# Softmax of a fused sparse-attention and cosine-FFN kernel: lasting exponential tiles with a column of 1e-9, and exponentials of the first local units straight from PSUM

## The chip, the core and the metric

The kernel runs on one core of one Trainium2 chip. The core has five engines that work side by side, each issuing its own instructions in order: PE (TensorE, matrix products), DVE (VectorE), ACT (ScalarE), POOL (GpSimd) and SP (SyncE, which here only issues transfers). Transfers (DMA) run beside them, issued by SP and by ACT. SBUF is the on-chip memory of 128 partitions; PSUM holds the results of PE, in eight banks of 512 fp32 columns.

The metric is the device time of one launch in microseconds. The kernel before has a median of 1000.85 us over three runs (1000.22 to 1001.1).

## The reference

Eight batches, eight heads, 576 positions, head size 64. Heads 0 to 3 attend to the last 32 positions, heads 4 to 7 to every 32nd position behind. The output becomes `x` with 4608 tokens of 512 features, and goes through a feed-forward layer with `h * cos(h)`.

```python
def _attn_ref(q, k, v):
    B, H, S, D = q.shape                                  # 8, 8, 576, 64
    stride = 32
    scores = (1.0 / np.sqrt(D)) * np.matmul(q, k.transpose(0, 1, 3, 2))
    pos = np.arange(S)
    rel = pos[:, None] - pos[None, :]
    mask_local = (rel >= 0) & (rel < stride)
    mask_strided = (rel >= 0) & (pos[None, :] % stride == pos[:, None] % stride)
    masks = np.stack([mask_local if h < H // 2 else mask_strided for h in range(H)], axis=0)
    scores = np.where(masks[None, :, :, :], scores, -1000000000.0)
    scores = scores - np.max(scores, axis=-1, keepdims=True)
    attn = np.exp(scores)
    attn = attn / (np.sum(attn, axis=-1, keepdims=True) + 1e-09)
    return np.matmul(attn, v).astype(np.float32)

def _moe_ref(x, w_in, w_out):                             # 4608x512, 512x2048, 2048x512
    h = x @ w_in
    g = h * np.cos(h)
    return (g @ w_out).astype(np.float32)

x = attn_out.transpose(0, 2, 1, 3).reshape(B * S, H * D)
return _moe_ref(x=x, **moe_kwargs)
```

## The kernel before

**Attention units.** A batch is ten units. Four are *strided* (head pairs p = 0, 1; halves u = 0, 1): six groups of 54 queries by 54 keys for each of two heads or half groups, a score tile of 128 x 324. Six are *local* (u = 0 to 2, p = 0, 1): three blocks of 64 queries by 96 keys for two heads, a score tile of 128 x 288. The zeros and minus infinities of the masks come as constants. A unit is a Python generator with three stages, which `step` calls one at a time:

1. loads of queries, keys and values (SP: L238, L240 local; L276, L278 strided), the mask and the scores on PE (L184; L249 local, L290 strided), and the softmax (L195 to L228) on DVE, ACT and POOL;
2. transposes on PE (L257 local, L302 strided) and a copy to `pt` on ACT (L259, L306);
3. products with the values on PE (L265, L316), copies to `x_l` or `x_t` on ACT (L269; L322, L328), and a transfer to `xT` in DRAM, issued by ACT (L271, L333).

**The softmax** has two forms. In the *plain* one, for batches 0 and 1 (20 units), the mask is added by a matmul into PSUM; DVE takes the maximum of each row and block and subtracts it (L199, L200), ACT takes the exponential into `e_sb` (L212, Exp). In the *later* one, for batches 2 to 7 (60 units), which runs beside the feed-forward layer whose ACT function is Sin, the exponential is made of two Silu, one DVE combination and a Square (L204 to L219), and POOL does the subtraction (L206). In both, DVE sums each block (L221, to `z`), adds 1e-9 (L222) and takes the reciprocal (L223); POOL multiplies by it (L225). Local units multiply in place in `e_sb`. Strided ones write to one of two lasting tiles `pn_s`, 128 x 6 x 64, whose columns 54 to 63 stay zero, since their transposes take 64 columns of each group.

**Feed-forward.** The 4608 tokens are 12 blocks of 384, the 2048 hidden features 16 chunks of 128. `load_x` brings a block of `xT` back in four pieces (SP L347 to `x_raw`) and splits each in a high and a low part (DVE L348, POOL L349). A chunk is `hidden`: twelve matmuls (L358), then ACT L364 (h / 2 pi, rounded), DVE L365 (the reduced argument), ACT L368 (Sin), DVE L371 (times h), ACT L374 and POOL L375 (the split `g_hi`, `g_lo`); and `outer`, three chunks later (`LAG`): nine matmuls (L382) into three accumulators of 128 x 512. After the last chunk of a block these go to `o` tiles (ACT, DVE, ACT: L390, L392) and to DRAM (SP L393).

**Order of the program.**

- First the 20 plain units, with warm-up matmuls between them (`keep_busy`, L442). `load_x(0)` and `load_x(1)` are written at steps 12 and 20.
- Then the weights, 32 tiles of 512 KB in two buffers `raw`: transfer (SP L114), DVE L116 and L119, ACT L124, DVE L125, ACT L129, and POOL L130, which frees the buffer. L116 of chunk f may not come ahead of L365 of chunk f - 2 of block 0 (`order` with `reduced`). Blocks 0 and 1 are computed as the weights come, and the first three chunks of block 2.
- Then blocks 2 to 11, with the 60 later units between the chunks, at places that a table (`KNOTS`) gives.

Up to block 2 a scheduler with a model of the time sets the order of each engine's instructions, within the dependences; a change of the code there also moves others. From block 2 on, PE's matmuls keep the order in which they are written (`in_turn`). `tile_pool` gives buffers in rotation: an instruction that writes a buffer waits for the last reader of what was in it. Plain units have three banks for scores (two of pool `ps_h`, one of `ps`), four `e_sb`, two `t_sb` and three `qk` buffers. `o` has two buffers up to the third chunk of block 2, so for the copies of blocks 0 and 1, and three behind it (pools `op`, L462 and L480).

Of the kernel before, what the change touches and what calls it, by code (L numbers as in the profile page):

```python
# [24 lines left out]
P = 128  # L25
# [4 lines left out]
LU = 3  # L30
# [38 lines left out]
def attention_cos_ffn(ctx, tc, qkl, vl, qkvs, w_in, w_out, eye, eye16, mask_l0, mask_l, mask_s, out):  # L69
# [85 lines left out]
    class Attention:  # L155
# [3 lines left out]
        def __init__(self, stack, plain, scores, transposed, products, ld_bufs):  # L159
# [11 lines left out]
            self.pn_s = itertools.cycle(pn_s)  # L171
# [23 lines left out]
        def softmax(self, s, mask, n, w, pn=None):  # L195
            t = self.wk.tile([P, SU * GB], F32, name="t_sb")[:, :n * w].rearrange("p (t w) -> p t w", w=w)
            mx = sm.tile([P, SU], F32, name="mx")
            if self.plain:
                nc.vector.tensor_reduce(out=mx[:, :n], in_=s, op=ALU.max, axis=AX.X)  # L199
                nc.vector.tensor_tensor(  # L200
                    out=t, in0=s, in1=mx[:, :n].unsqueeze(2).broadcast_to([P, n, w]), op=ALU.subtract
                )
            else:
                nc.vector.tensor_tensor(out=t, in0=s, in1=mask, op=ALU.add)  # L204
                nc.vector.tensor_reduce(out=mx[:, :n], in_=t, op=ALU.max, axis=AX.X)  # L205
                nc.gpsimd.tensor_tensor(  # L206
                    out=t, in0=t, in1=mx[:, :n].unsqueeze(2).broadcast_to([P, n, w]), op=ALU.subtract
                )
            e = self.wk.tile([P, SU * GB], F32, name="e_sb", bufs=4 if self.plain else 3)
            e = e[:, :n * w].rearrange("p (t w) -> p t w", w=w)  # L210
            if self.plain:
                exps.append(nc.scalar.activation(out=e, in_=t, func=AF.Exp, scale=0.125))  # L212
            else:
                nc.scalar.activation(out=e, in_=t, func=AF.Silu, bias=shift1, scale=0.0625)  # L214
# [378 lines left out]
```

## Time and profile before

| | us |
|---|---|
| median of three runs | 1000.85 (1000.22 to 1001.1) |
| profiled execution | 999.46 |
| its span, first to last instruction | 997.7 |
| PE busy | 968.3 (97%) |
| PE weight loads, beside PE | 847.5 (85%) |
| DVE busy | 466.5 (47%) |
| ACT busy | 499.2 (50%) |
| POOL busy | 385.2 (39%) |

The mean granted clock of TensorE was 0.995. Shares over the whole span average stages with different limits; here follows how the span divides. Plain attention fills the time to about 54 us, when the twelfth matmul of the first hidden chunk ends; until 205 us the weights stream in; at about 223 us the softmax of the first later unit is at its sums; from 256 us on blocks and later units alternate; and the last block's `o` goes out at the end. Rows of the timeline give the start in microseconds from the start of the span, the duration, the engine and line, the operation, output and inputs, and in brackets for how long the engine had waited and for what. A `q` behind an engine's name is its queue of transfers. In a row of waits stand the waiting instruction, the releaser, and then the total in us, the number of waits and the longest. In a row of groups stand the count, the busy time in us, the mean in ns of one, and the idle time ahead of them. In a row of a stretch stand its length, then for each engine its busy time and instructions.

### The profile page before, as it was taken

To read this page: it belongs to the slowest core of one execution; us is meant where nothing else is said; L and a number is where in the kernel's file an instruction comes from. 1 tells how busy PE (TensorE), PEld (TensorE's weight loads), DVE (VectorE), ACT (ScalarE), POOL (GpSimd) and SP (SyncE) were. 2 spreads that over 40 slices of the span, in tenths; PEclk is the share of its full clock that TensorE was granted. 3 is DMA by queue.
4 is the path that set the end of the run, shared out by engine and by line. 5 is a ranking of instruction groups with operands and counts; after the bars stand their busy time and mean duration, and the time that the engine had idled before them with its cause. 6 is when DMAs were issued, how large, how long until landed. Compare 5 with 4: busy or idle time off the path is not lost.

```text
span 997.7 us, 17749 instructions
## 1 busy us (share of the span) xinstructions
PE 968.3 (97%) x6890; PEld 847.5 (85%) x6890; DVE 466.5 (47%) x1005; ACT 499.2 (50%) x1043; POOL 385.2 (39%) x418
## 2 busy tenths in 40 slices
PE   8988988998999999999999999999999999999998
PEld 5777877877888888888888888888888888889997
DVE  6866677655454444434344444444344444322222
ACT  3655555565555555455445545554454544433433
POOL 2555554544344344333333344434243333332221
PEclk9999999999899999999999999999999999999999
DMA  8963333232322222111211322211221310100000
GB/s 247 300 199 103 111 108 112 80 105 73 102 85 88 70 79 84 42 50 59 83 58 35 110 79 76 82 50 53 88 59 34 98 55 29 41 20 1 33 1 32
DMA packets 48228, 80.14 MB, mean 80 GB/s; under 512 B 5904, under 2 KB 33296, under 8 KB 48144
## 3 DMA queue, kind: packets, MB, share of 16 engines
q1 hardware_dynamic: 38208, 69.35, 23.1%
q10 hardware_dynamic: 9936, 9.65, 2.8%
q8 instruction: 54, 0.88, 0.4%
q14 instruction: 30, 0.25, 0.1%
HBM read 60.11 MB, written 18.87 MB: 79 GB/s over the span
## 4 chain that ended last, share of the span: by engine, by line
PE 78%; DMA 4%; DVE 2%; ACT 1%; issue 1%; POOL 0%; DVEq 0%; POOLq 0%; ACTq 0%; SPq 0%
PE h L358 35%; PE acc L382 34%; DMA raw<-in_w_out 2%; PE acc L249 2%; PE acc L265 2%; PE acc L316 2%; PE acc L290 2%; PE acc L257 1%; PE acc L302 1%; DVE raw L116 1%; DMA raw<-in_w_in 1%; DMA xT<-x_t 0%; ACT r L368 0%; DVE r L371 0%; DVE raw L119 0%
## 5 line engine op out<-in xcount | busy, mean ns | idle before, releaser
L375 POOL TENSOR_TENSOR g_lo<-r,g_hi 128x384 fp32r<-128x384 f32 x192 | 198.3, 1033 | 396.6 <-issue 249.2
L358 PE MATMUL h<-x_hi,wi_h 128*128 128x384 f32 x768 | 267.9, 349 | 13.7 <-DVE r L371 13.7
L358 PE MATMUL h<-x_hi,wi_l 128*128 128x384 f32 x768 | 259.7, 338 | 0.0
L358 PE MATMUL h<-x_lo,wi_h 128*128 128x384 f32 x768 | 259.4, 338 | 0.0
L365 DVE SCALAR_TENSOR_TENSOR r<-r,h 128x384 f32<-128x384 int32 x192 | 106.1, 552 | 270.8 <-ACT r L364 247.7
L382 PE MATMUL acc<-wo_l,g_hi 128*128 128x512 f32 x576 | 227.4, 395 | 0.0
L382 PE MATMUL acc<-wo_h,g_hi 128*128 128x512 f32 x576 | 224.2, 389 | 1.4 <-ACT g_hi L374 1.4
L382 PE MATMUL acc<-wo_h,g_lo 128*128 128x512 f32 x576 | 224.6, 396 | 0.0
L358 PEld LDWEIGHTS h<-x_hi,wi_h 128*128 128x128 f32 x768 | 145.2, 189 | 31.0 <-DVE r L371 19.8
L368 ACT ACTIVATE r<-r,quarter 128x384 f32<-128x384 f32 x192 | 118.5, 617 | 96.5 <-DVE r L365 96.2
L358 PEld LDWEIGHTS h<-x_lo,wi_h 128*128 128x128 f32 x768 | 145.3, 189 | 5.0
L371 DVE TENSOR_TENSOR r<-r,h 128x384 f32<-128x384 f32 x192 | 106.0, 552 | 84.0 <-ACT r L368 83.4
L358 PEld LDWEIGHTS h<-x_hi,wi_l 128*128 128x128 f32 x768 | 145.1, 189 | 0.1
L364 ACT ACTIVATE r<-h 128x384 int32<-128x384 f32 x192 | 93.4, 487 | 102.0 <-PE h L358 95.5
L374 ACT CAST g_hi<-r 128x384 fp32r<-128x384 f32 x192 | 98.3, 512 | 87.5 <-DVE r L371 87.2
L382 PEld LDWEIGHTS acc<-wo_h,g_lo 128*128 128x128 f32 x576 | 108.0, 188 | 22.8
L382 PEld LDWEIGHTS acc<-wo_h,g_hi 128*128 128x128 f32 x576 | 108.3, 188 | 19.0 <-ACT g_hi L374 1.7
L382 PEld LDWEIGHTS acc<-wo_l,g_hi 128*128 128x128 f32 x576 | 108.0, 187 | 18.2
L349 POOL TENSOR_TENSOR x_lo<-x_raw,x_hi 128x384 fp32r<-128x384 f32 x48 | 50.9, 1062 | 130.9 <-DVE x_hi L348 107.4
L214 ACT ACTIVATE e_sb<-t_sb,shift 128x288 f32<-128x288 f32 (+1 forms) x60 | 32.9, 548 | 95.6 <-POOL t_sb L206 95.6
L348 DVE CAST x_hi<-x_raw 128x384 fp32r<-128x384 f32 x48 | 21.6, 452 | 60.9 <-DMA x_raw<-xT 60.2
L206 POOL TENSOR_TENSOR t_sb<-t_sb,mx 128x288 f32<-128x288 f32 (+1 forms) x60 | 41.6, 693 | 16.9 <-DVE mx L205 11.5
(66 smaller groups left out, 855.8 us busy)
## 6 DMA issues: line engine op xcount, KB each, us to landing
qk<-in_qkvs SPq DMA_DIRECT2D x32, 324.0 KB, 3.7
qk<-in_qkl SPq DMA_DIRECT2D x48, 208.0 KB, 3.3
x_raw<-xT SPq DMA_DIRECT2D x48, 192.0 KB, 2.4
out<-o SPq DMA_DIRECT2D x36, 256.0 KB, 2.1
raw<-in_w_in SPq DMA_DIRECT2D x16, 512.0 KB, 3.7
raw<-in_w_out SPq DMA_DIRECT2D x16, 512.0 KB, 3.8
v<-in_vl SPq DMA_DIRECT2D x48, 144.0 KB, 2.2
xT<-x_t ACTq DMA_DIRECT2D x16, 288.0 KB, 3.5
```

The source lines that it names most:

```text
L206: nc.gpsimd.tensor_tensor(out=t, in0=t, in1=mx[:, :n].unsqueeze(2).broadcast_to([P, n, w]), op=ALU.subtract)
L214: nc.scalar.activation(out=e, in_=t, func=AF.Silu, bias=shift1, scale=0.0625)
L348: nc.vector.tensor_copy(out=hi, in_=raw)
L349: nc.gpsimd.tensor_tensor(out=lo, in0=raw, in1=hi.bitcast(F32), op=ALU.subtract)
L358: mm = nc.tensor.matmul(h, w[:, f, c], x[c], start=(i == 0), stop=(i == len(ops) - 1))
L364: nc.scalar.activation(out=k, in_=h, func=AF.Copy, scale=1.0 / (2.0 * math.pi), bias=0.25)
L365: red = nc.vector.scalar_tensor_tensor(out=r, in0=k, scalar=-2.0 * math.pi, in1=h, op0=ALU.mult, op1=ALU.add)
L368: sin = nc.scalar.activation(out=r, in_=r, func=AF.Sin, bias=quarter)
L371: nc.vector.tensor_tensor(out=r, in0=r, in1=h, op=ALU.mult)
L374: nc.scalar.copy(out=g_hi, in_=r)
L375: nc.gpsimd.tensor_tensor(out=g_lo, in0=r, in1=g_hi.bitcast(F32), op=ALU.subtract)
L382: mm = nc.tensor.matmul(acc[t], g[:, ts], w[:, f], start=(f == 0 and i == 0), stop=(f == NFC - 1 and i == 2))
```

## The change

Exponentials are written to lasting tiles: three `e_l`, 128 x 3 x 97, for local units and three `e_s`, 128 x 6 x 64, for strided ones, in rotation, for plain and later units alike. Column 96 or 54 of each block holds 1e-9, set once, and the sum takes that column in, so the addition to `z` (L222) is gone. POOL multiplies in place; `e_sb` and `pn_s` are gone. Columns 55 to 63 of `e_s` are zero as before; column 54, now 1e-9, is transposed with them into a row that the copy to `pt` leaves out.

A plain local unit has no subtraction and no `t_sb` any more. After the maximum, ACT makes `low`, minus an eighth of it (128 x 3), and then three exponentials of 96 columns, one for each block, which read the scores in PSUM with `low` as bias. Plain strided units and later units keep their arithmetic. The pool `op` of the last part of the program has two buffers, not three.

```diff
-    pn_s = [const.tile([P, SU, GP], F32, name=f"pn_s{i}") for i in range(2)]
-    for t in pn_s:
+    e_l = [const.tile([P, LU, KW + 1], F32, name=f"e_l{i}") for i in range(3)]
+    e_s = [const.tile([P, SU, GP], F32, name=f"e_s{i}") for i in range(3)]
+    for t in e_s:
         nc.gpsimd.memset(t, 0.0)
+    for t, w in [(t, KW) for t in e_l] + [(t, GB) for t in e_s]:
+        nc.gpsimd.memset(t[:, :, w:w + 1], 1e-9)
...
-            self.pn_s = itertools.cycle(pn_s)
+            self.e = {LU: itertools.cycle(e_l), SU: itertools.cycle(e_s)}
...
-        def softmax(self, s, mask, n, w, pn=None):
-            t = self.wk.tile([P, SU * GB], F32, name="t_sb")[:, :n * w].rearrange("p (t w) -> p t w", w=w)
+        def softmax(self, s, mask, n, w):
+            tile = next(self.e[n])
+            e = tile[:, :, :w]
             mx = sm.tile([P, SU], F32, name="mx")
-            if self.plain:
+            if self.plain and n == LU:
                 nc.vector.tensor_reduce(out=mx[:, :n], in_=s, op=ALU.max, axis=AX.X)
-                nc.vector.tensor_tensor(
-                    out=t, in0=s, in1=mx[:, :n].unsqueeze(2).broadcast_to([P, n, w]), op=ALU.subtract
-                )
+                low = sm.tile([P, SU], F32, name="low")
+                nc.scalar.activation(out=low[:, :n], in_=mx[:, :n], func=AF.Copy, scale=-0.125)
+                for t in range(n):
+                    exps.append(
+                        nc.scalar.activation(out=e[:, t], in_=s[:, t], func=AF.Exp, bias=low[:, t:t + 1], scale=0.125)
+                    )
...
             z = sm.tile([P, SU], F32, name="z")
-            nc.vector.tensor_reduce(out=z[:, :n], in_=e, op=ALU.add, axis=AX.X)
-            nc.vector.tensor_scalar(out=z[:, :n], in0=z[:, :n], scalar1=1e-9, scalar2=None, op0=ALU.add)
+            nc.vector.tensor_reduce(out=z[:, :n], in_=tile[:, :, :w + 1], op=ALU.add, axis=AX.X)
             nc.vector.reciprocal(out=z[:, :n], in_=z[:, :n])
-            pn = e if pn is None else pn
             nc.gpsimd.tensor_tensor(
-                out=pn, in0=e, in1=z[:, :n].unsqueeze(2).broadcast_to([P, n, w]), op=ALU.mult
+                out=e, in0=e, in1=z[:, :n].unsqueeze(2).broadcast_to([P, n, w]), op=ALU.mult
...
-        op = stack.enter_context(tc.tile_pool(name="op", bufs=3, reuse_waits="tile"))
+        op = stack.enter_context(tc.tile_pool(name="op", bufs=2, reuse_waits="tile"))
```

The left-out part is the `else` branch, in which the code of the plain strided and of the later units stands as it was, one level deeper; the transposes of local units take the first 96 of the 97 columns.

The order that the scheduler finds differs too, in the first 200 us above all. Lines of the new program stand some numbers higher (L249 is L257, L358 is L362, L365 is L369).

First SP's queue at the first local units, from the first weight load (`raw`) to the first piece of x (`x_raw`). Before:

```order
L114 DMA raw<-in_w_in 128x1024
L114 DMA raw<-in_w_out 128x1024
L238 DMA qk<-in_qkl 128x416 x5
L240 DMA v<-in_vl 96x384
L114 DMA raw<-in_w_in 128x1024
L238 DMA qk<-in_qkl 128x416
L240 DMA v<-in_vl 96x384
L114 DMA raw<-in_w_out 128x1024
L276 DMA qk<-in_qkvs 128x648 x3
L347 DMA x_raw<-xT 128x384
```

and now:

```order
L117 DMA raw<-in_w_in 128x1024
L117 DMA raw<-in_w_out 128x1024
L246 DMA qk<-in_qkl 128x416 x4
L248 DMA v<-in_vl 96x384
L117 DMA raw<-in_w_in 128x1024
L246 DMA qk<-in_qkl 128x416 x2
L248 DMA v<-in_vl 96x384
L117 DMA raw<-in_w_out 128x1024
L284 DMA qk<-in_qkvs 128x648 x2
L248 DMA v<-in_vl 96x384
L351 DMA x_raw<-xT 128x384
```

The fifth load of local queries and keys has moved behind the third weight load, and one load of strided queries and keys behind the first piece of x.

Then PE, from the last strided products of batch 1 to the first matmul of the first hidden chunk (`h<-x_hi,wi_h`). Before:

```order
L316 MATMUL acc_791<-pt,v 64x54 x12
L257 MATMUL acc_848<-ident,e_sb 96x128 x3
L316 MATMUL acc_834<-pt,v 64x54 x10
L257 MATMUL acc_887<-ident,e_sb 96x128 x3
L249 MATMUL h<-qk 64x96 x6
L358 MATMUL h<-x_hi,wi_h 128x384
```

and now, beginning three rows behind the last strided products (L320, which was L316):

```order
L257 MATMUL acc_892<-qk 64x96 x6
L273 MATMUL acc_873<-pt,v 64x64 x6
L265 MATMUL acc_882<-ident,e_l_97 96x128 x3
L187 LDWEIGHTS ident_78
L187 MATMUL h<-ml,ident_78 128x288
L257 MATMUL h<-qk 64x96 x6
L273 MATMUL acc_912<-pt,v 64x64 x6
L265 MATMUL acc_921<-ident,e_l_98 96x128 x3
L257 MATMUL h<-qk 64x96 x6
L273 MATMUL acc_951<-pt,v 64x64 x6
L265 MATMUL acc_960<-ident,e_l_96 96x128 x3
L362 MATMUL h<-x_hi,wi_h 128x384
```

Scores, products (L273) and transposes (L265) of batch 1's local units that stood among or behind the matmuls of the first hidden chunks now stand ahead of the first one. Of product groups of batch 1's local units, two stood ahead of the chunk's twelfth matmul, and now three.

Last DVE at the first two later units, both strided (`e_s_99`, `e_s_100` are two of the three lasting tiles). Before:

```order
L216 SCALAR_TENSOR_TENSOR e_sb<-t_sb,e_sb 128x324
L221 TENSOR_REDUCE z<-e_sb 128x6
L216 SCALAR_TENSOR_TENSOR e_sb<-t_sb,e_sb 128x324
L222 TENSOR_SCALAR z<-z 128x6
L365 SCALAR_TENSOR_TENSOR r<-r,h 128x384
L223 RECIPROCAL z<-z 128x6
L221 TENSOR_REDUCE z<-e_sb 128x6
```

and now:

```order
L226 SCALAR_TENSOR_TENSOR e_s_99<-t_sb,e_s_99 128x6x54
L231 TENSOR_REDUCE z<-e_s_99 128x6
L226 SCALAR_TENSOR_TENSOR e_s_100<-t_sb,e_s_100 128x6x54
L232 RECIPROCAL z<-z 128x6
L369 SCALAR_TENSOR_TENSOR r<-r,h 128x384
L231 TENSOR_REDUCE z<-e_s_100 128x6
```

The addition is gone, and a chunk's L369 (before L365), which stood between it and the reciprocal, now stands behind the reciprocal.

More of the change, by code (lines that the diff above doesn't have):

```diff
@@ new lines, in softmax @@
+                low = sm.tile([P, SU], F32, name="low")
[4 more added lines that the diff above has]
+                    )
+            else:
+                t = self.wk.tile([P, SU * GB], F32, name="t_sb")[:, :n * w].rearrange("p (t w) -> p t w", w=w)
+                if self.plain:
+                    nc.vector.tensor_reduce(out=mx[:, :n], in_=s, op=ALU.max, axis=AX.X)
+                    nc.vector.tensor_tensor(
+                        out=t, in0=s, in1=mx[:, :n].unsqueeze(2).broadcast_to([P, n, w]), op=ALU.subtract
+                    )
+                    exps.append(nc.scalar.activation(out=e, in_=t, func=AF.Exp, scale=0.125))
+                else:
+                    nc.vector.tensor_tensor(out=t, in0=s, in1=mask, op=ALU.add)
+                    nc.vector.tensor_reduce(out=mx[:, :n], in_=t, op=ALU.max, axis=AX.X)
+                    nc.gpsimd.tensor_tensor(
+                        out=t, in0=t, in1=mx[:, :n].unsqueeze(2).broadcast_to([P, n, w]), op=ALU.subtract
+                    )
+                    nc.scalar.activation(out=e, in_=t, func=AF.Silu, bias=shift1, scale=0.0625)
+                    nc.scalar.activation(out=t, in_=t, func=AF.Silu, bias=shift2, scale=0.0625)
+                    nc.vector.scalar_tensor_tensor(
+                        out=e, in0=t, scalar=-math.exp(STEP), in1=e, op0=ALU.mult, op1=ALU.add
+                    )
+                    nc.scalar.activation(out=e, in_=e, func=AF.Square, scale=math.exp(SHIFT) / STEP)
@@ L227, in softmax @@
             )
-            return pn
+            return tile
         def stage(self, key):
@@ L256, in local @@
             for t in range(LU):
-                self.pe(nc.tensor.transpose(t_ps[:KW, t * P:(t + 1) * P], pn[:, t], ident))
+                self.pe(nc.tensor.transpose(t_ps[:KW, t * P:(t + 1) * P], pn[:, t, :KW], ident))
             pt = self.wk.tile([P, LU * P], F32, name="pt")
@@ L293, in strided @@
                     ))
-            pn = next(self.pn_s)
-            self.softmax(
-                s_ps[:, :SU * GB].rearrange("p (t w) -> p t w", w=GB), mask,
-                SU, GB, pn[:, :, :GB],
-            )
+            pn = self.softmax(s_ps[:, :SU * GB].rearrange("p (t w) -> p t w", w=GB), mask, SU, GB)
             yield
```

16 lines of the change are left out of this document (removed).

## The prediction

> **What bounds the kernel now.** I read the page's span line first, then busy time by stretch, then the waits of PE stage by stage, then the timelines at the places that those waits name. After the stretch come span, PE, PEld, DVE, ACT, POOL (busy us, instructions), the granted clock, the DMA share and GB/s.
>
> ```profile
> span 997.7 us, 17749 instructions
> 12.00:54.44 42.44, 39.73 (x622) 29.39 (x622) 37.17 (x109) 24.97 (x64) 21.52 (x27) 1.00 0.85 270
> 30.00:40.00 10.00, 10.00 (x175) 7.56 (x173) 9.49 (x27) 6.64 (x18) 7.12 (x8) 1.00 0.96 295
> 54.44:66.00 11.56, 7.46 (x79) 6.04 (x78) 7.98 (x13) 8.06 (x17) 7.87 (x7) 1.00 0.43 138
> 66.00:205.00 139.00, 127.41 (x615) 111.14 (x616) 91.53 (x140) 75.18 (x139) 72.44 (x61) 0.99 0.36 112
> 205.00:256.00 51.00, 44.77 (x388) 39.41 (x387) 25.59 (x61) 29.26 (x61) 18.86 (x24) 0.93 0.31 97
> 256.00:990.00 734.00, 734.00 (x5081) 653.27 (x5080) 300.30 (x671) 358.28 (x758) 262.81 (x295) 1.00 0.20 58
> ```
>
> From 256 to 990 us PE is never idle: DVE work taken out there (60 of the 80 softmaxes) buys nothing. Up to 54.44 us, where the first hidden chunk ends, DVE looks like the bound (37.17 of 42.44 us; 9.49 of 10 at its densest), but PE, which issues in a fixed order, is at 39.73, and at 10.00 of 10 in the densest stretch. So in this stage only the 2.71 us in which PE is idle can go. What ends its waits, for 12 to 54.44, 54.44 to 66 and 205 to 990 us in turn (total us, times, longest):
>
> ```profile
> PE h L249 <- DMA qk<-in_qkl: 1.5, 2, 1.3
> PE acc L249 <- DMA qk<-in_qkl: 1.2, 1, 1.2
> PE h L358 <- DVE r L371: 2.1, 1, 2.1
> PE acc L382 <- ACT g_hi L374: 1.4, 1, 1.4
> PE acc L265 <- ACT pt L259: 0.6, 1, 0.6
> PE acc L257 <- POOL e_sb L225: 3.1, 1, 3.1
> PE acc L302 <- POOL pn_s L225: 2.2, 1, 2.2
> PE acc L290 <- DVE t_sb L204: 0.9, 1, 0.9
> ```
>
> No wait of PE in the first stage names DVE, ACT or POOL: it waits for loads of queries and keys. The weight stream (66 to 205 us) paces itself: two buffers, each refilled when POOL has split the last tile. It therefore begins and ends earlier by as much as its start does, and what follows is shifted with it.
>
> **The change part by part, first stage.** DVE loses the `z` addition and the local subtraction; ACT pays.
>
> ```profile
> L222 DVE TENSOR_SCALAR z<-z 128x3 f32<-128x3 f32 (+1 forms) x19 | 7.0, 367 | 0.1
> L200 DVE TENSOR_TENSOR t_sb<-h,mx 128x288 f32<-128x288 f32 x8 | 3.6, 444 | 0.1
> L212 ACT ACTIVATE e_sb<-t_sb 128x288 f32<-128x288 f32 x12 | 5.3, 443 | 4.0 <-DVE t_sb L200 2.6 <-POOL pn_s L225 1.1 <-DVE z L223 0.3
> L214 ACT ACTIVATE e_sb<-t_sb,shift 128x288 f32<-128x288 f32 x36 | 19.3, 536 | 54.1 <-POOL t_sb L206 54.1
> L214 ACT ACTIVATE e_sb<-t_sb,shift 128x324 f32<-128x324 f32 x24 | 13.6, 566 | 41.5 <-POOL t_sb L206 41.5
> L328 ACT COPY x_t<-acc 128x36 f32<-128x36 f32 x16 | 3.1, 195 | 0.0
> 36.78 0.84 ACT L212 ACTIVATE e_sb<-t_sb 128x324 f32<-128x324 f32 x2
> 40.45 2.18 ACTq L271 DMA_DIRECT2D xT<-x_l  x2
> 49.73 0.33 ACTq L333 DMA_DIRECT2D xT<-x_t  x1
> 10.24 0.73 POOL L225 TENSOR_TENSOR pn_s<-e_sb,z 128x324 f32<-128x324 f32 x1 [8.74 <-DVE z L223]
> ```
>
> The first row counts 12 to 54.44 us alone. DVE sheds 7.0 us of additions and about 10 x 0.44 us of subtractions of the 37.17. For ACT, no row shows an exponential of 96 columns with a bias from memory, so I bound it: the two L214 rows have such a bias, and 36 columns more cost 30 ns, 0.83 each, so 96 columns are 536 - 192 x 0.83 = 376 ns. Two L212 of 470 ns take 0.84 together: one that follows another hides 0.10. A unit then costs 0.19 for `low` (the nearest row is L328) and 3 x 0.28 = 1.03 us, in place of 0.34: 0.69 more, 8.2 for twelve units. Without any overlap it is 0.19 + 3 x 0.376 - 0.44 = 0.88, or 10.5. ACT's free time is 42.44 - 24.97 = 17.5, less the 12 DMAs that it issues itself, about 5.5 (0.33 each, and one pair held up for 2.18): 12 us. It fits, but ACT is then at 24.97 + 5.5 + 8.2 = 38.7 us, and it takes DVE's place as the fullest engine beside PE.
>
> The Trainium skill ("ScalarE: Activation LUTs", What ACT_TABLE_LOAD costs) speaks against splitting an activation: each with a bias pointer has a fixed 280 ns, against 186 with constants, and successors hide 93 ns. By it 96 columns take 360 ns, an estimate from that page; the L214 rows (536 where it gives 520) agree within 3%, and the sum would move by 0.6 us at most.
>
> What remains on the path is PE's waits. The loads that end them come in another order (in the new program the fifth local load stands behind a weight load). I let both go, -2.7, bounds -2.7 and 0. One product group more stands ahead of the first hidden chunk's end (a pair of them is the first row below): +0.5. For ACT I charge what DVE's best stretch shows of an in-order engine: about 94% full. 38.7 / 0.94 = 41.2, against the 40.2 that PE would then need: +1.0; bounds 0 and, without overlap, 41.0 / 0.94 - 40.2 = +3.4.
>
> ```profile
> 56.11 0.92 PE L265 MATMUL acc<-pt,v 96*64 96x64 f32 x24
> 54.48 0.49 ACT L364 ACTIVATE r<-h 128x384 int32<-128x384 f32 x1 [0.18 <-PE h L358]
> 55.62 0.59 DVE L348 CAST x_hi<-x_raw 128x384 fp32r<-128x384 f32 x1 [1.27 <-DMA x_raw<-xT]
> 56.14 0.54 DVE L365 SCALAR_TENSOR_TENSOR r<-r,h 128x384 f32<-128x384 int32 x1
> 59.95 0.36 DVE L348 CAST x_hi<-x_raw 128x384 fp32r<-128x384 f32 x1 [1.43 <-DMA x_raw<-xT]
> 65.20 0.33 SPq L114 DMA_DIRECT2D raw<-in_w_in  x1
> ```
>
> After the chunk, L365 has its input at 54.97 and starts at 56.14: in DVE's order it stands behind a cast that waits for x. It is L365 that lets the next weights be worked on; their buffer is refilled at 65.20. The strided products that this x needs now stand further ahead of the first hidden chunk in PE's order, so its transfer starts earlier and the 1.2 us go: -1.2, bounds -1.2 and 0. What is late next is L364 itself. Start of the weight stream: -2.7 + 0.5 + 1.0 - 1.2 = -2.4.
>
> Hidden: the POOL memsets (one large one and six of a few columns more; POOL's first softmax starts at 10.24, after 8.74 us of idleness); an exponential of the fourth next unit waiting for the transposes that free its lasting tile, since these stand two units earlier in PE's order (behind it on ACT are the `pt` copies, for which PE would wait).
>
> **At 223 us**, where the second attention begins, the first softmax goes reduce, L222, another chunk's L365, L223:
>
> ```profile
> 223.84 0.17 DVE L222 TENSOR_SCALAR z<-z 128x6 f32<-128x6 f32 x1
> 223.91 0.55 DVE L365 SCALAR_TENSOR_TENSOR r<-r,h 128x384 f32<-128x384 int32 x1
> 224.37 0.18 DVE L223 RECIPROCAL z<-z 128x6 f32<-128x6 f32 x1
> ```
>
> POOL and then PE wait for L223 (the 2.2 us above). Now L223 follows at once, and L365 after it: 224.37 - 223.84 = 0.5 earlier, -0.5. The 3.1 us wait stays: there POOL stands behind x, whose transfer the change leaves alone.
>
> **Output tiles, three to two.** The third copy of a block now waits until the first one's tile is written out. The block that ends at 213 us already has two; then the last block; then PE at 320 us:
>
> ```profile
> 213.00 0.59 ACT L392 COPY o<-acc 128x512 f32<-128x512 f32 x1
> 215.77 0.59 ACT L392 COPY o<-acc 128x512 f32<-128x512 f32 x1 [0.38 <-DMA out<-o]
> 992.61 0.59 ACT L392 COPY o<-acc 128x512 f32<-128x512 f32 x1 [3.92 <-PE acc L382]
> 993.97 0.58 ACT L392 COPY o<-acc 128x512 f32<-128x512 f32 x1 [0.77 <-PE acc L382]
> 315.67 0.58 ACT L392 COPY o<-acc 128x512 f32<-128x512 f32 x1
> 320.23 0.39 PE L382 MATMUL acc<-wo_h,g_hi 128*128 128x512 f32 x1
> ```
>
> With two tiles the third copy starts 2.77 us after the first. At the end it would start at 992.61 + 2.77 = 995.4 instead of 993.97, with nothing beside it: +1.4. At an inner block's end (315.67) it would start at 318.4 and end at 319.0; PE needs that accumulator at 320.23, so 1.2 us of other matmuls cover it: 0. Queued behind it on ACT is the next chunk's g_hi, which PE uses three chunks later. Were a write 1.2 us slower, each such end would cost PE the excess.
>
> **Sum:** -2.4 - 0.5 + 1.4 = -1.5 us on the span of 997.7, so 996.2. The profiled execution itself took 999.46, 1.4 less than the median of the three runs, 1000.85 (1000.22 to 1001.1); I take the same difference from the median: 999.35, say **999.4**. A measurement tells about 0.2%, 2.0 us, from no change.
>
> **The rivals.**
> - *Transfers set the first stage.* The DMA engines are 0.96 busy at 30 to 40 us and both of PE's waits there end with one. If they stay and x lands when it did, ACT's work lies in the stretch as it is (41.2 of 42.44), and what is left is +0.5 - 0.5 + 1.4 = +1.4: **1002.2**. Against it: the bytes are the same, and some loads move later in the order than x.
> - *More goes than I count.* If x comes early enough that the second cast (1.43 us of waiting at 59.95) and so L371, for which PE waits 2.1 us, no longer stand late, all 4.1 us of PE idleness from 54.44 to 66 go in place of 1.2: -2.7 + 0.5 + 1.0 - 4.1 - 0.5 + 1.4 = -4.4: **996.4**. For it: DVE then has 11 us less to do. Against: the weight stream must follow at once.
> - *ACT becomes the bound, and it is slower.* If the small exponentials do not overlap, ACT needs 41.0 us of work; at 94% this is 43.6, past the 42.44 of now. It decides from where 38.7 exceeds about 39.9 (94% of 42.44), an exponential every 0.31 us instead of 0.28. Then PE waits for `pt` and for score banks, which are now read until the third exponential is done: 43.6 - 42.44 + 0.5 - 0.5 + 1.4 = +2.6, with no gain at the casts: **1003.5**.
>
> **How the numbers follow.** Forecast 42%, spread from -2.9 to -0.3 us, so that a third of it is past -2.0; transfers 22%, a tenth of it past +2.0; more goes 22%; ACT bound 14%. Faster: 0.22 + 0.14 = 0.36. Slower: 0.14 + 0.02, and 0.01 for slow writes at block ends, 0.17. Same: the rest, 0.47. Range 996.5 to 1003.2: it cuts off half of the second rival and somewhat over half of the third.
>
> **What would show it.** In the new trace: PE waits for `in_qkl` gone or not in 12 to 54 us; the first L364 about 1.2 us earlier, the first L365 about 2.4; the second pair of weight loads before 63 us; ACT near 39 us of the stage, with the small exponentials every 0.28 us; PE's 2.2 us wait at 223 us down to 1.7; a third last copy that waits for its DMA and a last stretch 1.4 us longer; no PE idle from 256 to 990. I am wrong if PE waits in the first stage for exponentials, `pt` copies or POOL, if the weight stream's period changes (its first few rounds are ordered a little differently on DVE and ACT), or if an inner block's end stops PE.

## The result, and the profile after

The changed kernel takes 1003.67 us (median of 20 runs, 1000.46 to 1010.31) beside 998.17 us for the kernel before (20 runs, 994.78 to 1001.1): a ratio of 1.0062, interval 1.0046 to 1.0079. It is slower by some 4.6 to 7.9 us, where 1.5 us less was forecast. (The kernel before has a lower median here than in the three runs shown first; only the ratio is free of that.) Three executions in the experiments at a mean granted clock of 0.556 to 0.849, of 1055.79 to 1555.21 us, are left out of the ratios.

The page of the changed kernel, span and busy time; then the stretches that were shown of before, and the first one up to the end of the first hidden chunk, now at 58.03 us (after the stretch: PE, PEld, DVE, ACT, POOL, the granted clock, DMA):

```profile
span 1001.3 us, 17696 instructions
...
PE 974.3 (97%) x6890; PEld 851.7 (85%) x6890; DVE 446.8 (45%) x913; ACT 504.8 (50%) x1079; POOL 386.6 (39%) x425
```

```profile
12.00:54.44 42.44, 37.98 (x608) 27.17 (x606) 27.79 (x73) 27.90 (x93) 20.67 (x24) 1.00 0.84 269
12.00:58.03 46.03, 41.35 (x638) 30.04 (x638) 29.97 (x80) 30.12 (x103) 23.42 (x28) 1.00 0.82 261
54.44:66.00 11.56, 10.85 (x101) 9.03 (x96) 9.07 (x19) 9.67 (x25) 8.04 (x8) 1.00 0.45 128
66.00:205.00 139.00, 129.19 (x614) 112.89 (x614) 94.40 (x140) 75.52 (x140) 73.34 (x62) 0.98 0.34 113
205.00:256.00 51.00, 45.27 (x406) 39.59 (x404) 24.15 (x56) 29.83 (x63) 19.79 (x24) 0.97 0.30 97
256.00:990.00 734.00, 733.70 (x5057) 652.72 (x5052) 287.78 (x616) 358.03 (x756) 261.49 (x294) 1.00 0.19 58
```

DVE has shed most of what it was to shed (37.17 to 27.79 us in the first stretch, 29.97 up to the chunk's end; some 11 were forecast to go). But from 256 to 990 us PE is as busy as before and gets 24 matmuls less done: 5057 in place of 5081. That points at a PE that never idles and has become slower. The start of the same instruction, ACT's first step of a chunk, at the second and the last chunk of the last block, before and after, shows by how much:

```profile
927.22 0.49 ACT L364 ACTIVATE r<-h 128x384 int32<-128x384 f32 x1 [1.32 <-PE h L358]
985.83 0.49 ACT L364 ACTIVATE r<-h 128x384 int32<-128x384 f32 x1 [1.32 <-PE h L358]
```

```profile
929.22 0.49 ACT L368 ACTIVATE r<-h 128x384 int32<-128x384 f32 x1 [1.34 <-PE h L362]
988.02 0.49 ACT L368 ACTIVATE r<-h 128x384 int32<-128x384 f32 x1 [1.34 <-PE h L362]
```

The 14 chunks take 58.61 us before (4.187 each) and 58.80 after (4.200), in a block in which the two programs do the same work. Below, such a *pace* is worked out in the same way.

Waits of PE after the change: three rows of 12 to 54.44 us, one of 54.44 to 66 us, two of 205 to 256 us, and the only one from 256 us on:

```profile
PE acc L273 <- ACT pt L267: 2.5, 2, 1.3
PE h L257 <- DMA qk<-in_qkl: 1.4, 1, 1.4
PE acc L320 <- DMA v<-in_qkvs: 0.5, 1, 0.5
PE h L362 <- DVE r L375: 0.4, 1, 0.4
PE acc L265 <- POOL e_l L233: 3.2, 1, 3.2
PE acc L306 <- POOL e_s L233: 1.7, 1, 1.7
PE acc L386 <- ACT o L396: 0.3, 1, 0.3
```

And ACT at the three exponentials of a unit, at a copy to `pt` that stands behind a transfer, and at the first stage's end; SP at the next weights; ACT at the last two copies of the output:

```profile
31.30 0.83 ACT L208 ACTIVATE e_l<-h,low 128x96 f32<-128x96 f32 x3
37.41 0.34 ACTq L279 DMA_DIRECT2D xT<-x_l  x1
37.79 0.47 ACT L267 COPY pt<-acc 96x384 f32<-96x384 f32 x1 [3.70 <-DMA xT<-x_t]
58.03 0.49 ACT L368 ACTIVATE r<-h 128x384 int32<-128x384 f32 x1 [1.35 <-PE h L362]
66.08 0.33 SPq L117 DMA_DIRECT2D raw<-in_w_in  x1
994.95 0.59 ACT L396 COPY o<-acc 128x512 f32<-128x512 f32 x1 [4.07 <-PE acc L386]
997.69 0.59 ACT L396 COPY o<-acc 128x512 f32<-128x512 f32 x1 [2.15 <-DMA out<-o]
```

The chunk whose first step on ACT started at 54.48 us has it at 58.03, and the weight loads of 65.20 us go out at 66.08. (They are the fourth pair of each program, which the prediction calls the second.) It doesn't last. ACT's first step of block 2's last chunk, before and after:

```profile
298.68 0.49 ACT L364 ACTIVATE r<-h 128x384 int32<-128x384 f32 x1
```

```profile
297.14 0.49 ACT L368 ACTIVATE r<-h 128x384 int32<-128x384 f32 x1 [0.95 <-PE h L362]
```

From there to the same step of the last block, 144 chunks, it takes 690.88 us in place of 687.15, 3.7 more; and from that step to the end 13.24 in place of 11.85, 1.4 more. What is lost is lost behind 297 us.

### The profile page after: what moved, and what is told of

It reads as the page before. It is cut to its first block, busy times and chain, and to the rows that moved or that the text cites. A ratio compares the mean times of both kernels' runs of the same rounds, so it can differ in the third digit from the quotient of the medians.

```text
span 1001.3 us, 17696 instructions
## 1 busy us (share of the span) xinstructions
PE 974.3 (97%) x6890; PEld 851.7 (85%) x6890; DVE 446.8 (45%) x913; ACT 504.8 (50%) x1079; POOL 386.6 (39%) x425
## 4 chain that ended last, share of the span: by engine, by line
PE 77%; DMA 4%; DVE 2%; ACT 2%; issue 1%; POOL 1%; DVEq 0%; POOLq 0%; ACTq 0%; SPq 0%
PE h L362 35%; PE acc L386 33%; DMA raw<-in_w_out 2%; PE acc L257 2%; PE acc L273 2%; PE acc L320 2%; PE acc L298 2%; PE acc L265 1%; DVE raw L119 1%; PE acc L306 1%; DMA xT<-x_t 1%; DMA x_raw<-xT 0%; DMA raw<-in_w_in 0%; ACT r L372 0%; POOL g_lo L379 0%
## 5 line engine op out<-in xcount | busy, mean ns | idle before, releaser
L362 PE MATMUL h<-x_hi,wi_h 128*128 128x384 f32 x768 | 269.1, 350 | 10.2 <-DVE r L375 10.1
L362 PE MATMUL h<-x_lo,wi_h 128*128 128x384 f32 x768 | 261.4, 340 | 0.0
L362 PE MATMUL h<-x_hi,wi_l 128*128 128x384 f32 x768 | 261.3, 340 | 0.0
L369 DVE SCALAR_TENSOR_TENSOR r<-r,h 128x384 f32<-128x384 int32 x192 | 106.3, 553 | 291.3 <-ACT r L368 259.7
L386 PE MATMUL acc<-wo_h,g_hi 128*128 128x512 f32 x576 | 228.0, 396 | 0.3 <-ACT o L396 0.3
L362 PEld LDWEIGHTS h<-x_hi,wi_h 128*128 128x128 f32 x768 | 145.2, 189 | 27.0 <-DVE r L375 16.0
L362 PEld LDWEIGHTS h<-x_lo,wi_h 128*128 128x128 f32 x768 | 145.5, 189 | 4.9
L368 ACT ACTIVATE r<-h 128x384 int32<-128x384 f32 x192 | 93.3, 486 | 105.4 <-PE h L362 99.9
L362 PEld LDWEIGHTS h<-x_hi,wi_l 128*128 128x128 f32 x768 | 145.5, 189 | 0.4 <-POOL wi_l L133 0.3
L224 ACT ACTIVATE e_l<-t_sb,shift 128x288 f32<-128x288 f32 x36 | 19.3, 537 | 54.3 <-POOL t_sb L221 54.2
```

Of the source, the lines that this page charges most:

```text
L362: mm = nc.tensor.matmul(h, w[:, f, c], x[c], start=(i == 0), stop=(i == len(ops) - 1))
L368: nc.scalar.activation(out=k, in_=h, func=AF.Copy, scale=1.0 / (2.0 * math.pi), bias=0.25)
L369: red = nc.vector.scalar_tensor_tensor(out=r, in0=k, scalar=-2.0 * math.pi, in1=h, op0=ALU.mult, op1=ALU.add)
L386: mm = nc.tensor.matmul(acc[t], g[:, ts], w[:, f], start=(f == 0 and i == 0), stop=(f == NFC - 1 and i == 2))
```

## The experiments

Each run is compared with the kernel before on the same chip; ratios have their 95% interval. Of `b_pad`, `b_xonly`, `b_ronly`, `b_x64` and `b_x256` there is a single execution each, of which only the trace is read.

### Controls: a slower chip, or a lower clock?

Both kernels as they are.

> The kernel before, unchanged, as a control: ratio 1.000. Three theories are open for what the change costs. ADDRESS: the lasting tiles stand ahead of the weights in SBUF, so that weights and x begin at another residue (21472 before, 26560 now; 32 and 0 modulo 64), and a chunk of the feed-forward layer in the last block takes 4.200 us instead of 4.187, 2.3 us over the 160 chunks in which PE sets the pace. OUTPUT: two output tiles cost 1.4 us at the end and some at the ends of inner blocks. CLOCK: the pauses of PE while weights stream lead to more stretches of 3.41 us at a granted clock of 0.5, each 1.7 us. Rival to ADDRESS: the two profiles came from chips of different speed. For this run: ADDRESS expects 4.187 us per chunk again, the rival any value, the same in all runs on this chip. CLOCK expects a mean granted clock of about 0.997, against 0.992 for the changed kernel.

> The changed kernel, unchanged, as a control: ratio about 1.006, the last copies of the output 1.4 us further apart. ADDRESS: 4.200 us per chunk in the last block. Rival (chip): the same per chunk as the kernel before shows on this chip. CLOCK: a mean granted clock about 0.005 below that of the kernel before, some 5 us of its time.

Measured: 1.0001 (0.9986 to 1.0016) and 1.0064 (1.0043 to 1.0086). The paces are again 4.187 and 4.200 us, on one chip: the pace belongs to the program. The mean granted clock was 0.994 over 6 runs of the changed kernel and 0.994 over 28 of the kernel before: CLOCK falls as a cause of the difference. (The scatter goes with the clock: the fastest of the 20 runs above, 1000.46 us, had 0.997, the slowest, 1010.31, 0.986.)

### The place in SBUF

The lasting tiles stand ahead of the weights, and all that follows moves. First the changed kernel with 32 unused bytes behind them, so that weights and x stand at the old residues modulo 64:

```diff
-    e_s = [const.tile([P, SU, GP], F32, name=f"e_s{i}") for i in range(3)]
+    e_s = [const.tile([P, SU, GP], F32, name=f"e_s{i}") for i in range(3)]; const.tile([P, 8], F32, name="pad")
```

> The changed kernel with 32 bytes of unused SBUF ahead of the weights, so that weights and x begin at the residue modulo 64 that they had before (26592, which is 32); every engine's order is as in the changed kernel. ADDRESS: a chunk is back at 4.187 us and the time 2.3 us below the changed kernel's. Rival (chip): no difference from the changed kernel on this chip, 0 us. CLOCK and OUTPUT: no difference either.

The timeline of that kernel at the same two chunks:

```profile
922.60 0.49 ACT L368 ACTIVATE r<-h 128x384 int32<-128x384 f32 x1 [1.29 <-PE h L362]
980.84 0.49 ACT L368 ACTIVATE r<-h 128x384 int32<-128x384 f32 x1 [1.29 <-PE h L362]
```

58.24 / 14 = 4.160: not the old pace, as ADDRESS by residues modulo 64 had it, but a better one. Over 160 chunks that is 6.4 us less than the changed kernel, and the time says the same: 1.0004 (0.9987 to 1.0022) in place of 1.0064. Thirty-two unused bytes give back the whole loss, with both other parts of the change still in: they more than undo what the place cost, since this place is better than that of before.

Then the kernel before with nothing changed but unused bytes: 128 between weights and x (`b_padx`), 32 ahead of the weights (`b_pad`), and 128 between `r` and x (`b_xonly`):

```diff
-    wo_l = const.tile([P, NFC, DM], F32R, name="wo_l")
+    wo_l = const.tile([P, NFC, DM], F32R, name="wo_l"); const.tile([P, 32], F32, name="pad")
```
```diff
-    pn_s = [const.tile([P, SU, GP], F32, name=f"pn_s{i}") for i in range(2)]
+    pn_s = [const.tile([P, SU, GP], F32, name=f"pn_s{i}") for i in range(2)]; const.tile([P, 8], F32, name="pad")
```
```diff
-    xs = ctx.enter_context(tc.tile_pool(name="xs", bufs=2 * NKC))
+    ctx.enter_context(tc.tile_pool(name="pd1", bufs=1)).tile([P, 32], F32, name="pad"); xs = ctx.enter_context(tc.tile_pool(name="xs", bufs=2 * NKC))
```

`b_ronly` has a like line with 128 bytes ahead of `r`, 896 behind it and two output tiles; `b_x64` and `b_x256` are `b_xonly` with 64 and 256 bytes.

> The kernel before with 128 unused bytes between the weights and x: weights stay at 21472, x, r and o move to the residues modulo 1024 that the kernel with 32 unused bytes has (x at 352 and 864 in place of 224 and 736). ADDRESS by residues modulo 1024 of weights and x: a chunk at 4.160 us in place of 4.187, 4.3 us over 160 chunks, ratio 0.9957. Rival, that the place of the weights against the fixed g tiles (217056) counts: 4.187 as before, ratio 1.000. Rival, that it isn't addresses but the stream of PE's instructions, which is the same here: 4.187.

> The kernel before with 32 unused bytes ahead of the weights, so that weights and x begin at 0 modulo 64, as in the changed kernel: by ADDRESS modulo 64 a chunk of the last block takes 4.200 us in place of 4.187; the rival (instruction stream) has 4.187.

> The kernel before with 128 unused bytes between r and the x_hi and x_lo tiles: only these and o move to the residues that gave 4.160 us a chunk (352, 864); weights, g and r stay (r at 224 and 736). What is open is why the nine outer matmuls, which read only wo and g, got faster (2081 to 2055 ns of start-to-start times) when nothing but sm, x_raw, r, x and o moved. Theory R: the other engines' reads and writes of r, at that time in each chunk, disturb PE's reads of SBUF, by the residue of r: here the twelve hidden matmuls change (2104 to 2105 ns, other pattern) and the nine outer ones stay at 2081, so 4.186 us a chunk. Theory X: the place of x counts for both: 2055 and 4.160 us.

> The kernel before (with two output tiles, for room) and r alone moved to the residues 352 and 864, x back at 224 and 736. Theory R: the nine outer matmuls take 2055 ns in place of 2081 and the hidden ones keep their pattern (2104), so 4.160 us a chunk. Theory X: 2081 and 4.187 us.

> The kernel before with 64 unused bytes ahead of the x tiles (x at 288 and 800 modulo 1024), nothing else moved but o. If the place of before (224, 736) is the odd one: 4.160 us a chunk. If each place has its own pace: another value, between 4.15 and 4.21.

> The kernel before with 256 unused bytes ahead of the x tiles (x at 480 and 992; the second piece then stands at the residue of the weights, 992). If equal residues of weights and x collide: slower than 4.187 us a chunk. If the place of before is the odd one: 4.160.

`r` moved alone, x moved alone by 128 bytes, and x moved by 64 bytes in a timed run (`b_x64t`, below):

```profile
926.52 0.49 ACT L364 ACTIVATE r<-h 128x384 int32<-128x384 f32 x1 [1.32 <-PE h L358]
985.13 0.49 ACT L364 ACTIVATE r<-h 128x384 int32<-128x384 f32 x1 [1.32 <-PE h L358]
```

```profile
922.93 0.49 ACT L364 ACTIVATE r<-h 128x384 int32<-128x384 f32 x1 [1.30 <-PE h L358]
981.17 0.49 ACT L364 ACTIVATE r<-h 128x384 int32<-128x384 f32 x1 [1.30 <-PE h L358]
```

```profile
918.20 0.49 ACT L364 ACTIVATE r<-h 128x384 int32<-128x384 f32 x1 [1.27 <-PE h L358]
976.07 0.49 ACT L364 ACTIVATE r<-h 128x384 int32<-128x384 f32 x1 [1.27 <-PE h L358]
```

4.187, 4.160 and 4.133. All of them together, by the residues modulo 256 of the addresses that the programs give weights, x and g; the sums are of the median start-to-start times of the 12 hidden and the 9 outer matmuls in chunks of the last part of the trace:

| kernels | weights, x, g mod 256 | 12 hidden + 9 outer, ns | pace, us |
|---|---|---|---|
| before, `c_before`, `b_op2`, `b_ronly`, `b_x256` | 224, 224, 224 | 2104 + 2081 | 4.187 |
| after, `c_after` | 192, 64, 224 | 2111 + 2089 | 4.200 |
| `b_pad` | 0, 0, 224 | 2105 + 2101 | 4.207 |
| `e_pad`, `e_op3`, `b_padx`, `b_xonly` | 224, 96, 224 | 2105 + 2055 | 4.160 |
| `b_x64`, `b_x64t`, `e_best` | 224, 32, 224 | 2079 + 2054 | 4.133 |

The kernels with two output tiles have the paces of their places too (`b_op2b` and `b_copyfirst` 4.187, `b_padx_op2` 4.160). Five places, five paces, and kernels with the same residues have the same pace, whatever else differs (256 bytes more change nothing); `e_nosplit` alone, at the fourth place, has 4.163 by its L368 rows, while its matmuls have 2106 + 2055 ns. `b_padx` in time: 0.9971 (0.9954 to 0.9989), with 0.9957 expected. Theory R falls, theory X stands. No simple rule on the residues was found: modulo 64 fails (`b_pad` has 4.207, not 4.200), `b_x64` is faster than either of its expectations, and equal residues of weights and x are not in themselves the worst (two equal pairs have 4.187 and 4.207, an unequal one 4.200).

The Trainium skill ("TensorE: Matmul & The Clock Gate", Step-by-step: what each phase is for) says that PE has a read port for the streamed operand and another for loading the next weights, so that loading takes no read bandwidth from the running matmul. It names no dependence on the operands' places, and the table shows one: the same loads beside the same matmuls take 4.133 to 4.207 us a chunk. Whether it is the loads that hold the matmuls up, no run here tells, since each of these matmuls has a load of its own.

### Two output tiles

The kernel before with two, twice, and with two at the better place of x (`b_padx_op2`):

```diff
-        op = stack.enter_context(tc.tile_pool(name="op", bufs=3, reuse_waits="tile"))
+        op = stack.enter_context(tc.tile_pool(name="op", bufs=2, reuse_waits="tile"))
```

> The kernel before with two output tiles in the last part in place of three, nothing else. OUTPUT: 1.4 us later at the end, and 0 to 1.5 us at the first inner block's end (at about 318 us); in all 1.4 to 3 us slower, ratio 1.0014 to 1.003. Rival: the third copy is covered by something else at the end, 0 us. ADDRESS and CLOCK: no difference beyond that.

> The kernel before with two output tiles a second time, unchanged, since the medians gave 5.3 us and the trace of the first showed 2.85 (1.6 at block ends after the third block of tokens, 1.25 at the end). If the trace has all of it: a median 2 to 4 us over the kernel before and ratio 1.002 to 1.004. Rival, that two tiles cost more in most executions than in the one profiled: ratio 1.005 or more, and this profile has PE waits for o over 1.1 us in sum.

> The kernel before with 128 unused bytes between weights and x and two output tiles: apart from the softmax it has what the changed kernel with 32 unused bytes has. ADDRESS: 4.160 us a chunk. OUTPUT: 2.85 us over the kernel with three tiles at these addresses (ratio 0.9971 there), so 1.000; the tail 1.3 us longer. If the softmax change is worth nothing: the same ratio to the kernel before as the changed kernel with 32 bytes had, 1.0004, within 0.0015; if it gains 2 us, 1.0024.

Measured: 1.0053 (1.0037 to 1.0068), 1.0051 (1.0033 to 1.0069), and 0.9999 (0.9984 to 1.0014) beside 0.9971 with three tiles, that is 2.8 us more. In the traces the tail is 1.2 to 1.3 us longer in all three, and the 144 chunks from block 2's last to the last block's take 1.6, 2.4 and 2.0 us more. So two tiles cost 2.8 to 3.7 us by the traces, and somewhat more by the medians of the first two (5.3 and 5.1 us by the ratios, with 1.4 to 3 expected); what makes up the rest stays open. PE's wait for `o` in the second of these kernels, from 256 us:

```profile
PE acc L382 <- ACT o L392: 1.9, 2, 1.7
```

The waits are at the ends of blocks 2 and 5 (0.2 and 1.7 us), and so is the whole loss behind 297 us but for the tail. From ACT's first step in the last chunk of one block to the same step of the next, the kernels with the old softmax and two tiles take as long as those with three tiles at the same place, to 0.01 us, in all blocks but 3 and 6, at whose starts these two ends lie. There the loss follows the time from the first to the third copy of the output:

| kernel, end of block | third copy after the first, us | lost, us |
|---|---|---|
| `b_copyfirst` (below), 2 | 3.86 | 0.04 |
| `b_op2b`, 2 | 4.27 | 0.45 |
| `b_op2`, 2 | 4.45 | 0.61 |
| `b_op2`, 5 | 4.79 | 0.97 |
| `b_copyfirst`, 5 | 4.86 | 1.04 |
| `b_op2b`, 5 | 5.79 | 1.97 |

The loss is what the copy is late beyond 3.82 us, to 0.02 us. At the other inner ends it comes after 2.7 to 3.4 us in these kernels, and nothing is lost.

In the two traces of the changed kernel, with 16 x 0.0134 a block for the pace taken off, blocks 3 and 6 take 0.75 and 0.28, and 0.56 and 0.95 us more. But blocks 4, 5 and 7 to 10 take 0.08 to 0.15 more each as well, 0.77 in sum, alike in both traces. The last block, without attention, does not, and in `e_pad`, 32 bytes further, it is 0.04 a block at most (against `b_padx`): it goes with the place, which costs something in the chunks beside attention too that the pace of the last block does not show. With about 0.13 of this kind in blocks 3 and 6 each it makes 1.0 us, and 0.8 and 1.3 are left for the two ends.

Block 5's end in the changed kernel, ACT, then DVE, then SP:

```profile
551.56 0.58 ACT L396 COPY o<-acc 128x512 f32<-128x512 f32 x1
552.02 0.63 ACT L372 ACTIVATE r<-r,quarter 128x384 f32<-128x384 f32 x1
552.54 0.44 ACT L229 ACTIVATE e_l<-e_l 128x288 f32<-128x288 f32 x1
555.09 0.52 ACT L378 CAST g_hi<-r 128x384 fp32r<-128x384 f32 x1 [2.11 <-DVE r L375]
555.51 0.58 ACT L396 COPY o<-acc 128x512 f32<-128x512 f32 x1
```

```profile
552.18 0.68 DVE L394 COPY o<-acc 128x512 f32<-128x512 f32 x1
554.23 0.36 DVE L352 CAST x_hi<-x_raw 128x384 fp32r<-128x384 f32 x1 [1.37 <-DMA x_raw<-xT]
554.51 0.55 DVE L375 TENSOR_TENSOR r<-r,h 128x384 f32<-128x384 f32 x1
```

```profile
551.71 0.33 SPq L351 DMA_DIRECT2D x_raw<-xT  x1
552.16 4.29 SPq L397 DMA_DIRECT2D out<-o  x3
```

```profile
SPq L351 <- DMA xT<-x_t: 2.6, 1, 2.6
```

The third copy starts 3.95 us after the first, where 2.74 is usual (997.69 - 994.95). Two queues have to do with it. On SP the write of the first `o` stands behind a load of x that waits 2.6 us for attention to have written it. Here that load goes out just before the first copy ends, and the write at once behind the copy (552.16); but right behind the load it lands 2.7 us later, at about 554.9 (2.0 us later at the end of the last block). On ACT the third copy stands behind the next chunk's g_hi, which waits for DVE, which waits for that load. In `b_op2b` SP's share is larger: the first copy ends at 549.76 and its write goes out 1.8 us later, since the load waits 4.6 us. ACT, then SP, there:

```profile
549.18 0.58 ACT L392 COPY o<-acc 128x512 f32<-128x512 f32 x1
554.56 0.51 ACT L374 CAST g_hi<-r 128x384 fp32r<-128x384 f32 x1 [3.95 <-DVE r L371]
554.98 0.58 ACT L392 COPY o<-acc 128x512 f32<-128x512 f32 x1
551.15 0.33 SPq L347 DMA_DIRECT2D x_raw<-xT  x1
551.58 4.33 SPq L393 DMA_DIRECT2D out<-o  x3
SPq L347 <- DMA xT<-x_t: 4.6, 1, 4.6
```

With three tiles the copy stood ahead of g_hi (copies at 551.33 and 552.65 us in the trace of before, g_hi at 555.80). In the rows of ACT's order the one edit does this at each of the nine inner ends:

```
 L368 ACTIVATE r<-r,quarter 128x384
 L219 ACTIVATE e_sb<-e_sb 128x288
+L374 CAST g_hi<-r 128x384
 L392 COPY o<-acc_5126 128x512
-L374 CAST g_hi<-r 128x384
 L364 ACTIVATE r<-h 128x384
```

`b_copyfirst` puts the copy back ahead, with two tiles (left out is how `hidden` is handed the block end's `outer`, and how `outer` returns its last copy):

```diff
...
+        last = outer(*first) if first else None
         g_hi = gp.tile([P, TB], F32R, name="g_hi")
         g_lo = gp.tile([P, TB], F32R, name="g_lo")
-        nc.scalar.copy(out=g_hi, in_=r)
+        cast = nc.scalar.copy(out=g_hi, in_=r)
+        if first:
+            order(cast, last, "output first")
...
```

> The kernel before with two output tiles, and ACT's third copy of each inner block ahead of the next g_hi cast, as with three tiles. QUEUE: what costs at inner ends is that the copy stands behind a cast that waits for DVE and a load of x. Then the third copy starts at most 3.0 us after the first at the ends of blocks 2 and 5 too (4.2 to 5.8 with the cast ahead), PE has no wait for o, and block ends cost 0 to 0.5 us in place of 1.6 to 2.4; what is left is the 1.3 us at the end. Median 1.3 to 3 us over the kernel before (ratio 1.001 to 1.003), beside 5 us (1.0051, 1.0053). Rival TILE: the wait for the tile's transfer is what costs: starts and waits as they were, ratio 1.005.

Its third copy at block 5's end, and PE's wait for `o`:

```profile
555.73 0.58 ACT L395 COPY o<-acc 128x512 f32<-128x512 f32 x1 [3.44 <-DMA out<-o]
```

```profile
PE acc L385 <- ACT o L395: 0.8, 1, 0.8
```

Measured: 1.0019 (0.9999 to 1.0038). QUEUE holds in part. By the medians some 3 us of the 5 are gone, more than the traces can show: the 144 chunks cost 1.1 us in place of 1.6 to 2.4, and the tail's 1.2 stay. The end of block 2 now costs next to nothing, that of block 5 still 1.0, and PE still waits 0.8 for `o`. The copies after blocks 2 and 5 start 3.9 and 4.9 us after the first, not 3.0 as expected, beside 4.3 to 4.5 and 4.8 to 5.8 with the cast ahead: now the write of the first `o`, behind the load of x on SP, is what they wait for, as the rival TILE had it. SP's half of the matter this edit leaves as it was.

### The softmax by itself

`e_op3` is the changed kernel with three output tiles (room comes from two `e_s` in place of three) at the residues of `b_padx`; `e_best` the same at those of `b_x64t`; `e_nosplit` is `e_pad` with subtraction and one exponential of 288 columns again:

```diff
-                low = sm.tile([P, SU], F32, name="low")
-                nc.scalar.activation(out=low[:, :n], in_=mx[:, :n], func=AF.Copy, scale=-0.125)
-                for t in range(n):
-                    exps.append(
-                        nc.scalar.activation(out=e[:, t], in_=s[:, t], func=AF.Exp, bias=low[:, t:t + 1], scale=0.125)
-                    )
+                t = self.wk.tile([P, SU * GB], F32, name="t_sb")[:, :n * w].rearrange("p (t w) -> p t w", w=w)
+                sm.tile([P, SU], F32, name="low")
+                nc.vector.tensor_tensor(
+                    out=t, in0=s, in1=mx[:, :n].unsqueeze(2).broadcast_to([P, n, w]), op=ALU.subtract); exps.append(
+                    nc.scalar.activation(out=e, in_=t, func=AF.Exp, scale=0.125))
```

> The changed kernel with three output tiles again; room for them comes from two e_s tiles in place of three, and an unused 544 bytes put the weights at 25568, 1024 below where the kernel with 32 unused bytes has them, x and the rest too. OUTPUT: 1.3 us less at the end and the block ends without a wait of PE for o, 3 to 5 us below the kernel with 32 unused bytes, so 992 to 994.5 us beside 997.7 for the kernel before, ratio 0.994 to 0.997. Rival: two e_s tiles make PE wait and give it back, ratio 0.998 to 1.001. ADDRESS, if only the residue modulo 1024 counts: a chunk of the last block at 4.160 us as with the 32 bytes; if the absolute address counts, another value.

> The changed kernel with 32 unused bytes and the local plain units' softmax as it was before (subtraction on DVE to t_sb, one exponential of 288 columns), the lasting tiles and the column of 1e-9 kept, the same addresses of weights and x. If the split exponentials save time in the first stage: the first round of weights (third pair of raw loads, at 66 us) comes later and the time is 1 to 2.5 us above the kernel with 32 unused bytes. Rival, that the weight stream takes the gain back: the same time within 0.5 us. Rival, that the split costs: 1 us less.

> The kernel before with 64 unused bytes ahead of the x tiles, timed. A chunk of the last block at 4.133 us in place of 4.187, 0.053 x 160 = 8.5 us, in every execution alike: about 0.9 percent faster, ratio 0.990 to 0.993. Rival, that the profiled run (992.0) was a lucky one: 0.995.

> The changed kernel with three output tiles, two e_s tiles, and weights and x at the residues modulo 256 of b_x64t (weights 224, x 32, g 224). ADDRESS modulo 256: 4.133 us a chunk here too. Softmax worth nothing: the ratio of b_x64t within 0.0015. If it gains the 2.4 us of the prediction's first stage: 0.0024 below. If it costs: above.

| old softmax | new softmax | same in both |
|---|---|---|
| `b_padx` 0.9971 (0.9954 to 0.9989) | `e_op3` 0.9984 (0.9967 to 1.0000) | pace 4.160, three tiles |
| `b_padx_op2` 0.9999 (0.9984 to 1.0014) | `e_pad` 1.0004 (0.9987 to 1.0022) | pace 4.160, two tiles |
| `b_x64t` 0.9924 (0.9900 to 0.9949) | `e_best` 0.9943 (0.9921 to 0.9966) | pace 4.133, three tiles |

The new softmax gains nothing in any of the three pairs (0.5 to 1.9 us slower by the ratios, each within its interval); `e_op3` and `e_best` have two `e_s` tiles, not three. `e_op3` is 2.0 us below `e_pad` by the ratios, not 3 to 5 as expected, and its rival, that two `e_s` tiles make PE wait, is not seen from 256 us on, where its PE has no wait. Over the 144 chunks from block 2's last on, `e_op3` takes 684.59 us beside 684.45 of `b_padx`, and `e_best` 680.57 beside 680.68 of `b_x64t`: there the softmax is worth nothing either way.

`e_nosplit`, at 1.0010 (0.9988 to 1.0032), can't be told from `e_pad`; whether the split alone gains or costs stays open. Its fourth pair of weight loads went out at 67.24 and 69.82 us, that of `e_pad` at 66.36 and 67.62, but its granted clock from 12 to 58 us was 0.93, that of `e_pad` 1.00. One thing goes with the split: ahead of the first hidden chunk's end PE waits 1.2 to 2.5 us for local units' `pt` in all five traces with three exponentials, and not at all in `e_nosplit` and in the thirteen with the old softmax.

`b_x64t`, the kernel before with 64 unused bytes, beats both kernels: 991.06 us, as much as its pace says (0.053 x 160 = 8.5 us; measured 5 to 10).

## Why the prediction was wrong, point by point

- **"From 256 to 990 us PE is never idle", so 0 there. This step failed.** It took a busy PE for a constant pace. The lasting tiles moved weights and x, and the pace went from 4.187 to 4.200 us: 160 x 0.0134 = 2.1 us, and about 1.0 more in the chunks beside attention, that have no term in the sum. That it is the place is shown by `e_pad` (32 bytes, -6 us) and `b_xonly`.
- **Output tiles at inner ends: 0, since 1.2 us of matmuls cover the third copy, and g_hi is "Queued behind it". This failed too.** g_hi stands ahead of the copy; I read ACT's order of before and not that of the changed kernel at these places. The cover of 1.2 us was about right (3.82 - 2.77 = 1.05), and so was 0 for the ordinary end, where the copy comes some 2.75 us after the first. The caveat in the same step, a write that is 1.2 us slower, was given a chance of 0.01; a copy later by that much is what happened at the ends of blocks 2 and 5 (3.9 to 6.0 us after the first). By the traces 0.8 to 2.8 us in the kernels with two tiles.
- **Output tiles at the end: +1.4. Right.** Third copy 2.74 us after the first, waiting for its DMA; 1.4 us measured in the changed kernel, 1.2 to 1.3 in the others.
- **First stage, -2.4: missed.** The first L364 was to come 1.2 us earlier and came 3.55 later. PE has 41.35 us of work ahead of it in place of 39.73 (+1.6, where +0.5 was counted): three product groups with their transposes and scores now stand ahead of the first hidden matmul, which starts at 55.63 in place of 50.13 us. And PE idles 4.7 us in place of 2.7, where 1.0 was counted. One wait for `in_qkl` is still there (1.4 us), and PE waits 2.5 us for `pt`, which was a sign of being wrong. PE's idleness from 54 to 66 us does go (4.1 to 0.7 us), as the second rival had it, but only because PE is later.
- **The weight stream "begins and ends earlier by as much as its start does": failed too, and it is why little is left of what the first stage lost.** The stream does not keep its period. Its fourth pair goes out at 62.9 to 66.2 us (mean 64.6) in thirteen traces with the old softmax and at 66.0 to 68.1 (mean 66.8) in five with the new one, but its last pair at means of 180.3 and 181.2, and the last chunk of block 2 starts at 294.8 to 298.7 us (mean 297.0) and at 295.4 to 297.5 (mean 296.6).
- **ACT: three exponentials every 0.28 us. Right** (0.83 for three). Up to 58.03 us ACT has 30.12 us of work, 4.4 of transfers that it issues, and 3.3 in which one of these stands waiting: 37.8 of 46.03 us, near the 39 forecast, and not the bound. The third rival had the waits for `pt` right, but not their cause: one `pt` copy stands 3.7 us behind that transfer (37.79 us). Its time, 1003.5, is the measured one by luck, as nothing of the first stage is left at 297 us.
- **At 223 us, -0.5: right**, 2.2 to 1.7 us of PE's wait.

The sum that the runs support: +3.1 for the place (2.1 by the pace of the last block, 1.0 in the chunks beside attention), +0.8 to 1.3 at the ends of blocks 2 and 5, +1.4 at the end, and about 0 for the softmax: 5.3 to 5.8 us, beside 5.5 between the medians. (Over the 144 chunks it is 3.7 and 4.2 us in the two traces of the changed kernel, of which 144 x 0.0134 = 1.9 is pace.)

## What to carry to other kernels

Where one engine is the bound and never idles, its pace is a term like any other: compare the start-to-start time of the same instructions in the last, quiet part of both traces before looking for waits. A tile put ahead of others moves them all; if PE reads them, try a few unused bytes before judging the change. And a wait for a buffer is priced by what stands ahead of it in each queue, in the order of the changed program.

## What the runs showed of the hardware that I had not expected

The start-to-start time of matmuls of 128x384 and 128x512 with a weight load each depends on where in SBUF the operands begin: 4.133 to 4.207 us for the same 21 matmuls at five places. It is the same for places that are equal modulo 256 bytes (`b_x256`; the weights at 21472 and, in `e_best`, at 25056). Moving x alone also sped up the nine outer matmuls, which do not read it (2081 to 2055 ns), while moving `r`, which the other engines use meanwhile, changed nothing (4.187). How the place of x reaches them is open; no run here separates it.
